# Attention scores and values in tiles of one shape: 64x32 for both, values in two banks

## The chip, the cores and the metric

The kernel runs on one core of a Trainium2 chip. Five engines work side by side, each through its own instructions in order: TensorE (PE in the profile; its weight loads are listed apart as PEld), VectorE (DVE), ScalarE (ACT), GpSimd (POOL) and SyncE (SP), which issues most DMAs. They meet at semaphores. TensorE writes its results to eight PSUM banks of 128 partitions x 512 f32; VectorE and ScalarE read them from there. The metric is the device time of one execution in microseconds, as the median of several runs.

## The reference

Two attention layers, a and b, of 32 heads of 20 features each over the same 2048 rows x of 640 features, with their own weights, and a gate for each row that mixes them.

```python
def _A_ref(x, wqkv, wo):
    B, S, D = x.shape            # 1, 2048, 640
    H = 32; Dh = D // H          # 20
    qkv = (lambda x, *d: x.transpose(*d))((x @ wqkv).reshape(B, S, 3, H, Dh), 2, 0, 3, 1, 4)
    q, k, v = qkv[0], qkv[1], qkv[2]
    scale = Dh ** -0.5
    scores = jnp.einsum("bhqd,bhkd->bhqk", q, k) * scale
    p = _softmax(scores, axis=-1)
    o = jnp.einsum("bhqk,bhkd->bhqd", p, v)
    return (lambda x, *d: x.transpose(*d))(o, 0, 2, 1, 3).reshape(B, S, D) @ wo
...
g = _sigmoid((x * gate_w).sum(-1, keepdims=True))
a = _A_ref(x, A_wqkv, A_wo)
b = _B_ref(x, B_wqkv, B_wo)
return g * a + (1 - g) * b
```

All inputs and the output are f32.

## The kernel before

The 64 heads of both layers go in 16 groups of four (GH = 4). For each group the queries come in four blocks of 512, and for each block the keys in eight pieces of 256: 16 x 4 x 8 = 512 steps. A group with a block of queries is called a unit here: eight steps.

In a step G the program does three kinds of work in turn, woven together by a string of letters (STEP, and LATE once no maxima are left):

- e: `scores` multiplies 128 keys of one head with 512 queries, in f16 (L696). Head j of a pair lies on partitions 64j to 64j + 63, so that two heads use the two row halves of TensorE, each product writing 128 partitions of one bank. ScalarE takes the exponential of the bank into an SBUF tile pt (L699). Eight products a step.
- m: `max_mm` computes scores once more, ahead of the steps (up to 15), the other way round: 128 queries with 512 keys, again f16 and on one row half (L638). VectorE reduces each bank to the largest score of each query (L649); for some of the products ScalarE first takes a positive part (L642) that VectorE then adds to the next bank while it reduces (L646). `finish_max` puts the negated maxima as extra rows beside the queries, so that the exponentials come out shifted. Eight products a step as well.
- V: `values` multiplies the weights pt of the step before, four heads, 128 keys, with the keys' values, in f32 (L714). Each head has 21 columns (20 features and a one, which sums the weights) and writes partitions 32h to 32h + 20 of the bank acc; the four heads lie side by side in four column tiles of TensorE. Two blocks V a step; acc gathers the 16 blocks of a unit.
- X: a slot for a piece of other work: projections of the next group, of the values, and of the output (`mms`, L426), with 128x128 tiles.

When a unit's last values are in, `take_acc` transposes acc on VectorE out of PSUM (L806), divides by the sum of weights (L811, L814), transposes back (L817) and stores the result in two f16 parts.

Of the eight banks one is acc, and seven (NB = 7) go in turns to everything else. `take` picks the one that is free first by a small clock in the program: `tick_score`, `tick_block` and `spend` carry an estimate of when TensorE, ScalarE and VectorE get to a piece of work, with T_SCORE for a pair of scores, T_VALUES for a block of values and T_MODE for what lies around a block. These numbers choose banks and nothing else; the order of the instructions is that of the program (manual_schedule), and each engine runs its own strictly in it.

Before the steps (now[0] < 0) the first group is projected and the maxima of its first two blocks of queries are computed.

Of the kernel before, what the change touches and what calls it, by code (L numbers as in the profile page):

```python
# [11 lines left out]
F32 = mybir.dt.float32  # L12
I32 = mybir.dt.int32
AF = mybir.ActivationFunctionType
OP = mybir.AluOpType
# [4 lines left out]
P = 128  # L20
# [4 lines left out]
NT = S // P  # L25
NC = D // P
GH = 4
NG = H // GH
GF = GH * DH
QB = 512  # L30
# [4 lines left out]
VW = DH + 1  # L35
# [23 lines left out]
AHEAD = 2  # L59
NB = 7  # L60

T_SCORE, T_MODE, T_VALUES, T_READY = 0.217, 0.1, 0.85, 0.39
T_EXP, T_MAX, T_BACK = 0.478, 0.6, 0.15
REST = 6
PRODUCT = "product"
# [6 lines left out]
def kernel(  # L72
# [10 lines left out]
    nc = tc.nc  # L83
# [7 lines left out]
    psum = ctx.enter_context(tc.tile_pool(name="psum", bufs=1, space=PSUM))  # L91
# [13 lines left out]
    QT = [consts.tile([P, 2, S], F16, name=f"qt{i}") for i in range(2)]  # L105
    KT = [consts.tile([P, 2, S], F16, name=f"kt{i}") for i in range(2)]

    KD = [consts.tile([P, 2, QB], F16, name=f"kd{i}") for i in range(2)]
    V = [consts.tile([P, NT, 2 * GH, VW], F32, name=f"v{i}") for i in range(2)]
    acc = psum.tile([P, QB], F32, name="acc")  # L110
    banks = [psum.tile([P, QB], F32, name=f"bank{i}") for i in range(NB)]
    gates = consts.tile([P, 2, NT], F32, name="gates")
    inv_x = consts.tile([P, 1], F32, name="inv_x")
    inv_g = consts.tile([P, 1], F32, name="inv_g")
# [16 lines left out]
    clock = {"pe": 0.0, "done": 0.0, "act": 0.0, "dve": 0.0}  # L131
    rows_free = [0.0, 0.0]
    block_end = [0.0, None]
    free_at, held = [0.0] * NB, set()
    now = [-1]
# [8 lines left out]
    def spend(engine, cost, ready=0.0):  # L144

        clock[engine] = max(clock[engine], ready) + cost
        return clock[engine] + T_BACK
# [5 lines left out]
    def tick_score(j, i):  # L153

        clock["pe"] = max(clock["pe"], rows_free[j], free_at[i])
        rows_free[j] = clock["pe"] + T_SCORE
        return clock["pe"] + T_READY

    def tick_block(cost, ready=0.0):

        begin = block_end[0] if now[0] < 0 and block_end[1] == rows_free else max(rows_free) + T_MODE
        clock["pe"] = max(begin, ready)
        rows_free[:] = [clock["pe"] + cost + T_MODE] * 2
        block_end[:] = [clock["pe"] + cost, list(rows_free)]
        clock["done"] = clock["pe"] + cost + T_READY - T_MODE
# [298 lines left out]
    def run(gen):  # L464
        for _ in gen:
            pass
# [142 lines left out]
    mparts, ready = {}, set()  # L609
# [12 lines left out]
    def max_mm(u, ch, heads=(0, 1)):  # L622

        g, qb, i = unit_of(u)
        pair, t = divmod(i, 4)
        if (g, qb) not in mparts:
            max_parts(g, qb)  # L630
        q0 = qb * QB + t * P
        for j in heads:
            two = u < AHEAD * NS or ch < 2 and (j == 0 or g == 0)
            i, pt = take()
            ready = tick_score(j, i)
            r = slice(64 * j, 64 * j + 60)
            k = KD[g % 2 if ch == 0 else 1][r, pair] if two and ch % 2 == 0 else KT[g % 2][r, pair, ch * QB:(ch + 1) * QB]
            nc.tensor.matmul(pt, QT[g % 2][r, pair, q0:q0 + P], k, start=True, stop=True)  # L638
            m = mparts[g, qb][:, pair, j, t, ch:ch + 1]
            if two and ch % 2 == 0:  # L640
                relus[u, j] = start.tile([P, QB], F32, name="rl0", bufs=4) if u < AHEAD * NS else work.tile([P, QB], F32, name="rl", bufs=2)
                nc.scalar.activation(relus[u, j], pt, AF.Relu)  # L642
                back = relu_at[u, j] = spend("act", T_EXP, ready)
            elif two:
                rl = relus.pop((u, j))
                nc.vector.tensor_tensor_reduce(rl, pt, rl, 1.0, LOW, OP.add, OP.max, m)  # L646
                back = spend("dve", T_MAX, max(ready, relu_at.pop((u, j))))
            else:
                nc.vector.tensor_reduce(m, pt, axis=AX.X, op=OP.max)  # L649
                back = spend("dve", T_MAX, ready)  # L650
            give(i, back)
# [26 lines left out]
    ptiles, weighed = {}, {}  # L678
# [9 lines left out]
    def scores(G, kk, pair, heads=(0, 1)):  # L688

        g, qb, i = unit_of(G)  # L690
        kt = 2 * i + kk
        for j in heads:
            i, et = take()
            ready = tick_score(j, i)
            r = slice(64 * j, 64 * j + 64)
            nc.tensor.matmul(et, KT[g % 2][r, pair, kt * P:(kt + 1) * P],  # L696
                             QT[g % 2][r, pair, qb * QB:(qb + 1) * QB], start=True, stop=True)
            pt = pp.tile([P, QB], F32, name="pt")
            nc.scalar.activation(pt, et, AF.Exp, scale=factor(g // 4))  # L699
            ptiles[G, kk, 2 * pair + j] = pt  # L700
            weighed[G, kk] = spend("act", T_EXP, ready)
            give(i, weighed[G, kk])
# [5 lines left out]

    def values(G, kk):
        g, qb, i = unit_of(G)  # L710
        tick_block(T_VALUES, weighed.pop((G, kk)))
        kt = 2 * i + kk
        for h in range(GH):
            nc.tensor.matmul(acc[32 * h:32 * h + VW, :], V[(g // 2) % 2][:, kt, (g % 2) * GH + h, :],  # L714
                             ptiles.pop((G, kk, h)), start=(kt == 0), stop=(kt == NT - 1))


    wo_parts = {}
# [83 lines left out]
    def take_acc(g, qb):  # L802


        turned = work.tile([P, QB], F32, name="ot", bufs=2)
        nc.vector.transpose(turned, acc)  # L806
        spend("dve", T_MAX)
        few, many = (2, 8) if g == 2 * NG - 1 else (6, 16)
        sq = work.tile([P, 16], F32, name="sq", bufs=2)
        t3 = turned.rearrange("p (b e) -> p b e", e=32)  # L810
        nc.vector.reciprocal(sq, t3[:, :, DH])  # L811
        spend("dve", 0.25)
        yield from turns(few)
        nc.gpsimd.tensor_tensor(t3, t3, sq.unsqueeze(2).to_broadcast([P, 16, 32]), op=OP.mult)  # L814
        yield from turns(many)
        ot = work.tile([P, QB], F32, name="ob", bufs=1)
        nc.vector.transpose(ot, turned)  # L817
        spend("dve", T_MAX)
        o = work.tile([P, 2, QB], F16, name="on", bufs=2)
        nc.gpsimd.tensor_copy(o[:, 0], ot)  # L820
        nc.gpsimd.tensor_tensor(o[:, 1], ot, o[:, 0], op=OP.subtract)
        if g < 2 * NG - 1:
            yield from turns(16)
            for h in range(GH):
                f = (g % NG * GH + h) * DH
                nc.sync.dma_start(o_scr[g // NG][:, f:f + DH, qb * QB:(qb + 1) * QB].rearrange("k d q -> d k q"),
                                  o[32 * h:32 * h + DH])
            stored.add((g, qb))
        else:
            last.append((qb, o))  # L830
# [16 lines left out]
    def take_last():  # L847

        ot = work.tile([P, QB], F32, name="ot", bufs=2)
        nc.scalar.activation(ot, acc, AF.Copy)  # L850
        i, pt = take()
        one = ident.rearrange("p (h e) -> p h e", e=32)[:, :, DH]
        for t in range(4):
            nc.tensor.matmul(pt[:, 4 * t:4 * t + 4], ot[:, t * P:(t + 1) * P], one, start=True, stop=True)
        busy(2)
        rc = work.tile([P, 16], F32, name="sq", bufs=2)
        nc.vector.reciprocal(rc, pt[:, :16])
        give(i, spend("dve", 0.3))
        i, pt = take()
        nc.tensor.transpose(pt[:16, :P], rc, ident)  # L860
        busy(2)
        rt = wts.tile([16, P], F32, name="rt", tag="rt", bufs=1)
        nc.scalar.activation(rt, pt[:16, :P], AF.Copy)
        give(i, spend("act", 0.3))
        o = work.tile([P, 2, QB], F16, name="on", bufs=2)
        rows_of = picks[0].rearrange("p k e -> p (k e)")
        spreads = []
        for t in range(4):
            spreads.append(take())
            nc.tensor.matmul(spreads[t][1][:, :P], rows_of[:, t * P:(t + 1) * P], rt, start=True, stop=True)  # L870
# [46 lines left out]
    start = start_stack.enter_context(tc.tile_pool(name="start", bufs=1))  # L917
# [3 lines left out]
    zeros = start.tile([P, QB], F16, name="zeros")  # L921
    nc.gpsimd.memset(zeros, 0.0)

    def clear(n):

        for _ in range(n):
            nc.tensor.matmul(acc, zeros[:, :P], zeros, start=True, stop=True)  # L927

    w_t = wqkv[0].rearrange("(c p) f -> p c f", p=P)
    for i in range(0, NT, 2):  # L930
# [164 lines left out]
    for block in range(AHEAD):  # L1095
# [7 lines left out]
            advance()  # L1103
        run(finish_max(0, block))
    run(rest)
    start_stack.close()

    pp = ctx.enter_context(tc.tile_pool(name="pp", bufs=12))
# [213 lines left out]
```

## Time and profile before

| | before |
|---|---|
| median of 3 runs | 2743.3 us (2743.12 to 2743.63) |
| span of the profiled execution | 2741.6 us |
| TensorE's granted clock | 1.00 in nearly all of the span |
| matmuls and weight loads in the trace | 23333 each |
| DMA | 46 GB/s on average |

Of the profiled execution the page gives the span, from its first to its last instruction; the runs' time includes what lies around it.

Times in the profile are in microseconds, and means of one instruction in ns. A row of groups reads: line, engine, operation, out<-in, shapes, count, then after the bar the time in which at least one of them ran, the mean length of one, and the idle time of the engine just before them with what ended it. In a timeline a row is start, length and what, with x8 for eight of a kind run together. An f32 product of the program stands in the trace as two matmuls and two weight loads. Matmuls overlap: one of 512 columns is listed with 0.38 us, though the next one in the same place can start after about 0.22.

The stages of the span: the start; from 103.6 us, the first block of values, the 512 steps, 468 of them between 190 and 2600 us; from 2665.6 us, the last reduction of maxima, steps without maxima until 2727.5 us; and the end.

### The profile page before, as it was taken

To read this page: it belongs to the slowest core of one execution; us is meant where nothing else is said; L and a number is where in the kernel's file an instruction comes from. 1 tells how busy PE (TensorE), PEld (TensorE's weight loads), DVE (VectorE), ACT (ScalarE), POOL (GpSimd) and SP (SyncE) were. 2 spreads that over 40 slices of the span, in tenths; PEclk is the share of its full clock that TensorE was granted. 3 is DMA by queue.
4 is the path that set the end of the run, shared out by engine and by line. 5 is a ranking of instruction groups with operands and counts; after the bars stand their busy time and mean duration, and the time that the engine had idled before them with its cause. 6 is when DMAs were issued, how large, how long until landed. Compare 5 with 4: busy or idle time off the path is not lost.

```text
span 2741.6 us, 62441 instructions
## 1 busy us (share of the span) xinstructions
PE 2725.5 (99%) x23333; PEld 940.2 (34%) x23333; DVE 2426.1 (88%) x4712; ACT 2533.9 (92%) x5149; POOL 699.6 (26%) x1010
## 2 busy tenths in 40 slices
PE   9999999999999999999999999999999999999999
PEld 4433333333333332333333333333333333333222
DVE  8789999999999999888888998989988888999992
ACT  4999999999999999999999999999999999999997
POOL 6232222222223422312221121223342212211111
PEclk9999999999999999999999999999999999999999
DMA  4021102010120211102012230221201112122112
GB/s 144 17 59 24 31 15 44 7 33 14 25 55 20 61 45 51 39 9 61 20 49 53 67 85 25 60 57 47 67 17 42 29 51 64 32 77 62 49 49 77
DMA packets 175401, 125.59 MB, mean 46 GB/s; under 512 B 103672, under 2 KB 145456, under 8 KB 175096
## 3 DMA queue, kind: packets, MB, share of 16 engines
q1 hardware_dynamic: 172552, 120.31, 17.2%
q8 instruction: 182, 2.98, 0.4%
q0 software_dynamic: 1600, 0.96, 0.3%
q14 instruction: 123, 1.01, 0.1%
q10 hardware_dynamic: 944, 0.33, 0.0%
HBM read 55.53 MB, written 31.86 MB: 32 GB/s over the span
## 4 chain that ended last, share of the span: by engine, by line
PE 96%; ACT 1%; DVE 1%; issue 0%; DMA 0%; POOL 0%; POOLq 0%; SPq 0%; ACTq 0%; DVEq 0%
PE acc L714 36%; PE bank L426 21%; PE bank L638 20%; PE bank L696 18%; ACT pt L699 1%; DVE mpart L649 1%; PE bank L895 0%; PE bank L956 0%; PE acc L927 0%; DMA xs<-in_A_x_dram 0%; DVE rl L646 0%; ACT rl L642 0%; DVE ot L806 0%; POOL xx L899 0%; POOL on L875 0%
## 5 line engine op out<-in xcount | busy, mean ns | idle before, releaser
L699 ACT ACTIVATE pt<-bank 128x512 f32<-128x512 f32 x4096 | 2167.1, 613 | 125.8 <-PE bank L696 91.6
L649 DVE TENSOR_REDUCE mpart<-bank 128x1 f32<-128x512 f32 x2944 | 1842.2, 681 | 227.3 <-PE bank L638 122.7
L714 PE MATMUL acc<-pt,v 128*21 128x512 f32 x8192 | 1081.7, 600 | 0.1
L696 PE MATMUL bank<-qt,kt 64*128 64x512 f16 x4096 | 1035.2, 380 | 1.4 <-ACT pt L699 0.9
L638 PE MATMUL bank<-kt,qt 60*128 60x512 f16 x3520 | 1006.7, 380 | 1.4 <-ACT pt L699 0.2
L638 PEld LDWEIGHTS <-qt 60*128 60x128 f16 x4096 | 237.9, 94 | 896.7 <-issue 829.3
L646 DVE CUSTOM_DVE_ANT_0 rl<-bank,rl 128x512 f32<-128x512 f32 x576 | 386.5, 677 | 7.2 <-ACT rl L642 2.8
L642 ACT ACTIVATE rl<-bank 128x512 f32<-128x512 f32 x576 | 339.0, 598 | 7.3 <-PE bank L638 6.7
L714 PEld LDWEIGHTS acc<-pt,v 128*21 128x21 f32 x8192 | 143.0, 99 | 429.5 <-issue 426.5
L696 PEld LDWEIGHTS <-kt 64*128 64x128 f16 x4096 | 229.4, 94 | 174.1 <-issue 64.1
L426 PE MATMUL bank<-xx,wbh 128*128 128x168 f16 (+3 forms) x2480 | 286.4, 236 | 0.6 <-DVE xx L961 0.3
L426 PE MATMUL bank<-xx,wbl 128*128 128x168 f16 (+3 forms) x1240 | 257.5, 235 | 0.0
L426 PEld LDWEIGHTS <-wbh 128*128 128x128 f16 x2480 | 192.5, 98 | 110.2 <-issue 104.6
L814 POOL TENSOR_TENSOR ot<-ot,sq 128x512 f32<-128x512 f32 x63 | 66.1, 1049 | 574.7 <-DVE sq L811 539.4
L638 PE MATMUL bank<-kd,qt 60*128 60x512 f16 x576 | 203.4, 379 | 0.8
L426 PE MATMUL bank<-woh,o_in 128*128 128x320 f16 (+3 forms) x700 | 157.7, 290 | 0.0
L426 PE MATMUL bank<-wvh,xx 128*128 128x160 f16 (+1 forms) x1280 | 156.6, 234 | 0.0
L455 POOL CAST cq<-fs 128x512 f16<-128x512 f32 x60 | 36.7, 611 | 459.9 <-ACT fs L453 459.9
L426 PEld LDWEIGHTS <-xx 128*128 128x128 f16 x1920 | 131.1, 97 | 59.0 <-issue 56.2
L426 PE MATMUL bank<-wvl,xx 128*128 128x160 f16 (+1 forms) x640 | 137.7, 232 | 0.0
L426 PEld LDWEIGHTS <-wbl 128*128 128x128 f16 x1240 | 121.2, 98 | 4.7 <-issue 1.3
L426 PEld LDWEIGHTS <-o_in 128*128 128x128 f16 (+1 forms) x1050 | 87.3, 97 | 91.0 <-issue 68.5
(156 smaller groups left out, 1288.6 us busy)
## 6 DMA issues: line engine op xcount, KB each, us to landing
y_scr<-y_out SPq DMA_DIRECT2D x48, 320.0 KB
y_out<-y_scr SPq DMA_DIRECT2D x32, 320.0 KB
kt<-cq SPq DMA_DIRECT2D x120, 80.0 KB
o_scr<-on SPq DMA_DIRECT2D x240, 40.0 KB
o_in<-o_scr SPq DMA_DIRECT2D x64, 96.0 KB
kt<-cq SPq DMA_DIRECT2D x136, 40.0 KB
wstage<-in_B_wqkv_dram SPq DMA_DIRECT2D x13, 400.0 KB
xs<-in_A_x_dram SPq DMA_DIRECT2D x8, 640.0 KB
```

Source lines behind the costliest of these rows:

```text
L426: nc.tensor.matmul(out_ap, a, b, start=(k == 0), stop=(k == len(pairs) - 1))
L455: nc.gpsimd.tensor_copy(hi, f)
L638: nc.tensor.matmul(pt, QT[g % 2][r, pair, q0:q0 + P], k, start=True, stop=True)
L642: nc.scalar.activation(relus[u, j], pt, AF.Relu)
L646: nc.vector.tensor_tensor_reduce(rl, pt, rl, 1.0, LOW, OP.add, OP.max, m)
L649: nc.vector.tensor_reduce(m, pt, axis=AX.X, op=OP.max)
L696: nc.tensor.matmul(et, KT[g % 2][r, pair, kt * P:(kt + 1) * P], QT[g % 2][r, pair, qb * QB:(qb + 1) * QB], start=True, stop=True)
L699: nc.scalar.activation(pt, et, AF.Exp, scale=factor(g // 4))
L714: nc.tensor.matmul(acc[32 * h:32 * h + VW, :], V[(g // 2) % 2][:, kt, (g % 2) * GH + h, :], ptiles.pop((G, kk, h)), start=(kt == 0), stop= ...
L814: nc.gpsimd.tensor_tensor(t3, t3, sq.unsqueeze(2).to_broadcast([P, 16, 32]), op=OP.mult)
```

## The change

The scores of the steps (both kinds, e and m) are written as four products of 32 columns of the stationary operand instead of one of 128, so that they run in tiles of 64 rows x 32 columns. The values' products are cut into two halves of 64 keys; the first half gathers in accs[0], the second in accs[1], so values run in 64x32 tiles too. At the end of a unit ScalarE copies accs[1] to SBUF, VectorE adds accs[0] to it, and the rest of take_acc follows. accs[1] is the seventh of the other banks until the steps begin; from then on six banks are left for the rest. The program's clock gets a new tick for values, without T_MODE.

```diff
-T_SCORE, T_MODE, T_VALUES, T_READY = 0.217, 0.1, 0.85, 0.39
+T_SCORE, T_MODE, T_VALUES, T_READY = 0.217, 0.1, 0.86, 0.39
...
-    acc = psum.tile([P, QB], F32, name="acc")
-    banks = [psum.tile([P, QB], F32, name=f"bank{i}") for i in range(NB)]
+    accs = [psum.tile([P, QB], F32, name=f"acc{i}") for i in range(2)]
+    banks = [psum.tile([P, QB], F32, name=f"bank{i}") for i in range(NB - 1)] + [accs[1]]
...
+    def product_of_score(pt, stationary, moving):
+
+        if now[0] < 0:
+            nc.tensor.matmul(pt, stationary, moving, start=True, stop=True)
+            return
+        for c in range(0, P, 32):
+            nc.tensor.matmul(pt[c:c + 32], stationary[:, c:c + 32], moving, start=True, stop=True)
+
+    def tick_values(ready):
+
+        clock["pe"] = max(max(rows_free), ready)
+        rows_free[:] = [clock["pe"] + T_VALUES] * 2
+        clock["done"] = clock["pe"] + T_VALUES + T_READY
...
-            nc.tensor.matmul(pt, QT[g % 2][r, pair, q0:q0 + P], k, start=True, stop=True)
+            product_of_score(pt, QT[g % 2][r, pair, q0:q0 + P], k)
...
-            nc.tensor.matmul(et, KT[g % 2][r, pair, kt * P:(kt + 1) * P],
-                             QT[g % 2][r, pair, qb * QB:(qb + 1) * QB], start=True, stop=True)
+            product_of_score(et, KT[g % 2][r, pair, kt * P:(kt + 1) * P], QT[g % 2][r, pair, qb * QB:(qb + 1) * QB])
...
-        tick_block(T_VALUES, weighed.pop((G, kk)))
+        tick_values(weighed.pop((G, kk)))
         kt = 2 * i + kk
-        for h in range(GH):
-            nc.tensor.matmul(acc[32 * h:32 * h + VW, :], V[(g // 2) % 2][:, kt, (g % 2) * GH + h, :],
-                             ptiles.pop((G, kk, h)), start=(kt == 0), stop=(kt == NT - 1))
+        pts = [ptiles.pop((G, kk, h)) for h in range(GH)]
+        for k, acc in enumerate(accs):
+            r = slice(64 * k, 64 * k + 64)
+            for h in range(GH):
+                nc.tensor.matmul(acc[32 * h:32 * h + VW, :], V[(g // 2) % 2][r, kt, (g % 2) * GH + h, :], pts[h][r],
+                                 start=(kt == 0), stop=(kt == NT - 1))
...
+        total = work.tile([P, QB], F32, name="ob", bufs=1)
+        nc.scalar.activation(total, accs[1], AF.Copy)
+        back = spend("act", T_EXP)
+        nc.vector.tensor_tensor(total, accs[0], total, op=OP.add)
+        spend("dve", T_MAX, back)
         turned = work.tile([P, QB], F32, name="ot", bufs=2)
-        nc.vector.transpose(turned, acc)
+        nc.vector.transpose(turned, total)
...
-        nc.scalar.activation(ot, acc, AF.Copy)
+        nc.scalar.activation(ot, accs[1], AF.Copy)
+        nc.vector.tensor_tensor(ot, accs[0], ot, op=OP.add)
...
+    held.add(NB - 1)
+    nc.tensor.matmul(accs[1], zeros[:, :P], zeros, start=True, stop=True)
     start_stack.close()
```

On TensorE, at a block of values in the middle of the program, the order before is this (names: qt queries, kt keys, v values; a score of kind m, the block with its four heads in one row, then scores of both kinds):

```order
L638 LDWEIGHTS qt_80
L638 MATMUL bank_92<-kt_82,qt_80 128x512
L714 MATMUL acc<-pt,v_87 21x512 x4
L638 LDWEIGHTS qt_80
L638 MATMUL bank_89<-kt_82,qt_80 128x512
L696 LDWEIGHTS kt_82
L696 MATMUL bank_90<-qt_80,kt_82 128x512
```

and with the change, at a like place (L165 is the line in product_of_score; acc_88 and acc_89 are the two banks of values):

```order
L165 LDWEIGHTS qt_80
L165 MATMUL bank_95<-kt_82,qt_80 32x512
L730 MATMUL acc_88<-pt,v_87 21x512 x4
L730 MATMUL acc_89<-pt,v_87 21x512 x4
L165 LDWEIGHTS qt_80
L165 MATMUL bank_90<-kt_82,qt_80 32x512
L165 LDWEIGHTS qt_80
L165 MATMUL bank_90<-kt_82,qt_80 32x512
```

Nothing changed its place; each score is four weight loads and four matmuls into quarters of its bank, one behind the other (the first two of bank_90 are shown), and the block of values has eight products instead of four.

On VectorE, around the end of a unit before, with what each waits for (L649 and L646 are maxima, L806 the transpose of acc):

```order
L649 TENSOR_REDUCE mpart<-bank_93 128x1 [waits PE_49]
L646 ISA rl,mpart<-bank_89,rl 128x512 [waits DVE_49,PE_49]
L646 ISA mpart 128x1
L806 STREAM_TRANSPOSE ot<-acc 128x512 [waits PE_49]
L811 RECIPROCAL sq<-ot 128x16 [waits DVE_49]
L649 TENSOR_REDUCE mpart<-bank_94 128x1 [waits PE_49]
```

and with the change (L824 is the sum):

```order
L660 ISA rl,mpart<-bank_90,rl 128x512 [waits DVE_49,PE_49,Activation_49]
L660 ISA mpart 128x1
L824 TENSOR_TENSOR ob<-acc_88,ob 128x512 [waits Activation_49]
L827 STREAM_TRANSPOSE ot<-ob 128x512 [waits DVE_49]
L832 RECIPROCAL sq<-ot 128x16 [waits DVE_49]
L663 TENSOR_REDUCE mpart<-bank_91 128x1 [waits PE_49]
```

The sum stands ahead of the transpose and waits for ScalarE where the transpose waited for TensorE. On ScalarE the copy has come between the exponentials (L712) at the same unit end:

```order
L712 ACTIVATE pt<-bank_95 128x512 [waits PE_49,Activation_49]
L712 ACTIVATE pt<-bank_93 128x512 [waits DVE_49,PE_49]
L822 ACTIVATE ob<-acc_89 128x512 [waits PE_49,Pool_49]
L712 ACTIVATE pt<-bank_94 128x512 [waits DVE_49,PE_49]
L712 ACTIVATE pt<-bank_92 128x512 [waits PE_49,Activation_49]
```

It waits for the unit's last values on TensorE, and everything behind it on ScalarE waits with it. SyncE and GpSimd have the same instructions in the same order as before.

More of the change, by code (lines that the diff above doesn't have):

```diff
@@ L926, in clear @@
         for _ in range(n):
-            nc.tensor.matmul(acc, zeros[:, :P], zeros, start=True, stop=True)
+            nc.tensor.matmul(accs[0], zeros[:, :P], zeros, start=True, stop=True)
     w_t = wqkv[0].rearrange("(c p) f -> p c f", p=P)
```

## The prediction

> **What bounds the kernel now.** I read the page first (span, busy time, the chain that ended last), then what TensorE waited for between 190 and 2600 us, where nearly all steps lie.
>
> ```profile
> span 2741.6 us, 62441 instructions
> ...
> PE 2725.5 (99%) x23333; PEld 940.2 (34%) x23333; DVE 2426.1 (88%) x4712; ACT 2533.9 (92%) x5149; POOL 699.6 (26%) x1010
> ...
> PE 96%; ACT 1%; DVE 1%; issue 0%; DMA 0%; POOL 0%; POOLq 0%; SPq 0%; ACTq 0%; DVEq 0%
> ...
> PE bank L696 <- ACT pt L699: 0.6, 2, 0.3
> ```
>
> The last row is the whole answer of the waits of PE in that window: 0.6 us in 2410. TensorE waits for nobody, and its own sequence sets the time. A busy PE is not a PE at its peak, though, so the next question is what its microseconds hold. The chain, piece by piece in order of time, shows one period of a step (start, length, what):
>
> ```profile
> 1199.12 0.99 PE acc L714 x8
> 1200.10 0.32 PE bank L638
> 1200.42 0.22 PE bank L696 x2
> 1200.64 0.00 PE bank L638
> 1200.64 0.22 PE bank L696 x2
> 1200.86 0.99 PE acc L714 x8
> ```
>
> Values take 0.99 us, the first pair of scores behind them 0.32, each later pair 0.22; the period is 1.74. To see what these would be without interruption I take a stretch of back-to-back matmuls of 512 columns from the start of the program:
>
> ```profile
> 11.16 10.52 PE L927 MATMUL acc<-zeros 128*128 128x512 f16 x48
> ...
> L927 PE MATMUL acc<-zeros 128*128 128x512 f16 x56 | 12.6, 379 | 0.0
> ```
>
> (10.52 - 0.38)/47 = 0.216 us for 512 f16 columns. A pair of scores, two row tiles side by side, is at that rate already. Values are two f32 passes, and eight records in two rounds of four:
>
> ```profile
> 1199.49 0.61 PE L714 MATMUL acc<-pt,v 128*21 128x512 f32 x4
> 1200.79 0.14 PEld L714 LDWEIGHTS acc<-pt,v 128*21 128x21 f32 x8 [0.43 <-issue]
> 1200.79 1.06 PE L714 MATMUL acc<-pt,v 128*21 128x512 f32 x8
> ```
>
> 1.06 - 0.61 = 0.45 us from round to round, so a pass costs about two columns' time per column, 2 x 0.216 = 0.43, and a block of values should be 0.86. Three pairs and one block should be 3 x 0.216 + 0.86 = 1.51 us; they take 1.74. **0.23 us per block of values is lost** where the array goes from 64x128 tiles to 128x32 tiles and back.
>
> Is that loss due to the tile shape, or to f16 against f32? The products of a projection are f16, as scores are, in one 128x128 tile:
>
> ```profile
> 1334.20 0.38 PE L638 MATMUL bank<-kt,qt 60*128 60x512 f16 x1
> 1334.51 0.24 PE L426 MATMUL bank<-wvh,xx 128*128 128x160 f16 x1
> ...
> 1335.43 0.23 PE L426 MATMUL bank<-wvl,xx 128*128 128x160 f16 x1
> 1335.50 0.23 PE L426 MATMUL bank<-wvh,xx 128*128 128x160 f16 x1
> 1335.66 0.39 PE L696 MATMUL bank<-qt,kt 64*128 64x512 f16 x1
> ```
>
> Score to projection 0.31 instead of 0.22, projection to score 0.16 instead of 0.07: 0.09 at each edge with one data type on both sides. So it is the shape.
>
> **The change part by part.** *Removed: the two edges of each block of values.* Scores and values both run in 64x32 tiles, so 0.23 us go at each of 8192/8 = 1024 blocks (L714's count in the period above, x8 each). I take 0.22, since eight tiles start one after the other: 0.02 us for four in the x4 row (0.61 against one matmul's 0.59 to 0.60), 0.007 each. 1024 x 0.22 = 225 us. TensorE alone would end at 2741.6 - 225 = 2517 us.
>
> *Split scores.* Sixteen score products of a step become 64. What I need is that four column tiles stream side by side at full rate. Values show it: four streams of 512 x 4 bytes in 0.43 us; four f16 streams of 512 x 2 bytes in 0.216 us are the same rate. A pair in 64x32 tiles is not in the trace. Lower bound: 0.216, nothing lost. Upper bound: the starts of eight tiles add to each round, 8 x 0.007 = 0.05, so 0.27; eight pairs a step then cost 0.4 us more, 512 x 0.4 = 205 us, which eats the gain: 2722. I take the lower end, because the second round of values follows the first after 0.45 with the starts of four tiles inside it.
>
> *Split values.* Two halves of 64 keys in two banks: eight products per block in place of four, but on eight tiles at once, 0.86 again. Bounds 0.86 to 0.86 + 4 x 0.007.
>
> *What is late next.* Without TensorE's edges the two engines behind it are close. The counts of the window 190 to 2600 us, and the time from one instruction to the next where they run back to back:
>
> ```profile
> L699 ACT ACTIVATE pt<-bank 128x512 f32<-128x512 f32 x3743 | 1983.7, 611 | 114.7 <-PE bank L696 82.3 <-PE bank L638 9.3
> L649 DVE TENSOR_REDUCE mpart<-bank 128x1 f32<-128x512 f32 x2805 | 1754.3, 681 | 205.2 <-PE bank L638 103.9 <-PE bank L696 96.5
> L714 PE MATMUL acc<-pt,v 128*21 128x512 f32 x7484 | 988.5, 600 | 0.0
> L646 DVE CUSTOM_DVE_ANT_0 rl<-bank,rl 128x512 f32<-128x512 f32 x469 | 316.6, 675 | 0.7 <-ACT pt L699 0.4 <-PE bank L638 0.2
> L642 ACT ACTIVATE rl<-bank 128x512 f32<-128x512 f32 x468 | 279.1, 596 | 0.9 <-PE bank L638 0.8
> L453 ACT ACTIVATE fs<-bank 128x128 f32<-128x128 f32 (+2 forms) x226 | 71.2, 315 | 15.8 <-issue 4.5 <-PE bank L426 3.3
> L806 DVE STREAM_TRANSPOSE ot<-acc 128x512 f32<-128x512 f32 x58 | 41.4, 714 | 3.4
> L817 DVE STREAM_TRANSPOSE ob<-ot 128x512 f32<-128x512 f32 x59 | 41.3, 699 | 0.0
> ...
> 511.43 1.09 ACT L699 ACTIVATE pt<-bank 128x512 f32<-128x512 f32 x2 [0.25 <-PE bank L696]
> 504.67 2.48 DVE L649 TENSOR_REDUCE mpart<-bank 128x1 f32<-128x512 f32 x4 [0.23 <-PE bank L638]
> ```
>
> 7484/16 = 468 steps in 2410 us, 5.15 each. TensorE would need 2410 - 936 x 0.22 = 2204. ScalarE: 1.09 - 0.61 = 0.48 per full tile, 4211 x 0.48 = 2021, with L453 and some 60 us of smaller groups about 2152. VectorE: (2.48 - 0.68)/3 = 0.60, 2805 x 0.60 + 317 + 83 = 2083, with some 75 us of smaller groups about 2158. Both stand within 3% of the new TensorE time, so the step comes near a balance of three engines, where each one's uneven moments reach the others.
>
> *Added.* At each of 63 unit ends (take_acc) a ScalarE copy of a bank, price 0.48 to 0.60 (L642, L699), and a VectorE sum of a bank and an SBUF tile. The trace has no such sum; between the 0.60 of a reduction and the 0.71 of L806 I take 0.68, as L646 reads the same two kinds of operand. That makes ScalarE about 2180 and VectorE about 2198 in the window. The sum waits for the copy and the copy for the values: behind the copy on ScalarE stand the exponentials of the next scores, behind the sum on VectorE the transpose, the reciprocal and the maxima. The next unit's first values wait for the sum. Does this reach TensorE? Before, at one unit end:
>
> ```profile
> 1201.92 0.72 DVE L806 STREAM_TRANSPOSE ot<-acc 128x512 f32<-128x512 f32 x1
> ...
> 1204.41 1.06 PE L714 MATMUL acc<-pt,v 128*21 128x512 f32 x8
> ```
>
> Values begin at 1200.79, VectorE reads them at 1201.92 and is done at 1202.64; the next values at 1204.41 leave 1.8 us. After: copy until 1202.5, sum until 1203.2, next values about 0.4 earlier, at 1204.0. Cover 0.8 us; it costs nothing while ScalarE is less than that behind.
>
> *Six banks in place of seven.* A unit end hands VectorE, beyond its maxima, the sum 0.68 and two transposes 1.4, with the small reductions about 2.6 us in one or two steps; spare time is some 0.1 us a step. What the banks do not absorb, TensorE waits. Lower end 0, upper end 63 x 2.6 = 164 us; there is no row that decides, and I take the middle, 82.
>
> *The sum:* 2517 + 82 = 2599 against the span of 2741.6. The runs' median is 2743.3, 1.7 us more, which lie around the span; as a run's time that is **2601**.
>
> **The rivals.** *The engines behind take most of it.* Same mechanism, nothing absorbed: 2517 + 164 = 2681. For it: one bank fewer, and three engines within about 1%. Against: the reductions' 205 us of idle time now.
>
> *The edges stay*, because a change from f16 to f32 within one shape drains too. Copies and sums lie beside TensorE, so about 2742. Against it: the 0.09 at f16 edges, the same size as half of 0.23.
>
> *Slower: TensorE's instructions come too slowly.* The place is the issue of weight loads and matmuls. A step now has 2 x (16 + 16 + 12.7) = 89 records in 5.15 us, and then 2 x (64 + 32 + 12.7) = 217, which in 4.7 us is one per 21.7 ns. In bursts TensorE does far better (eight weight loads in 0.14 us, each 0.10 long), but the densest longer stretch I find is this one, with 15 matmuls and 15 weight loads:
>
> ```profile
> 191.47 0.27 PE L426 MATMUL bank<-xx,wbh 128*128 128x128 f16 x2
> ...
> 192.25 0.22 PE L426 MATMUL bank<-xx,wbl 128*128 128x128 f16 x1
> ```
>
> 0.78 us for 30 records, 26 ns each, and there the columns set the pace. If 26 ns were the rate of issue, a step would be 217 x 0.026 = 5.64 us, 0.49 over 5.15: 2742 + 512 x 0.49 = 2993. It decides from 5.15/217 = 23.7 ns on. For it: nothing in this trace is that dense for long. Against it: the bursts.
>
> The Trainium skill, "TensorE: Matmul & The Clock Gate", Part 2, has a rule of this kind: where firmware and not the hardware decoder handles matmuls, each takes about 62 ns. By it a step's 64 + 16 + 12.7 = 93 matmul instructions would take 5.75 us, an estimate from that page, and the kernel about 3050. No row here shows which way matmuls are decoded.
>
> **How the numbers follow.** Forecast 2601: 0.58, own range 2520 to 2660. Engines behind, 2681: 0.16. Edges stay, or the split scores eat the gain, 2722 to 2742: 0.06, mostly within 0.2%. Issue, 2993: 0.20. Faster by over 0.2%: 0.58 + 0.16 + 0.01 = 0.75; within 0.2%, about what a measurement of this kernel tells from no change: 0.04; slower: 0.21. The range goes from 2520 (no wait behind TensorE) to 2760 (edges stay, and some waits); it leaves out the issue case, 0.20.
>
> **What would show it.** Right: in the chain, values and the pair behind them come to about 1.1 us in place of 1.31, pairs stay at 0.22, and waits of PE for banks appear, some 80 us, most near unit ends. ScalarE's and VectorE's shares rise to about 95%. Wrong: pairs longer than 0.24 with no wait named (tiles or issue); values over 0.95 with scores on both sides (the edge is not the shape); waits of PE above 160 us (balance worse than any unit end explains); values at unit ends waiting for the sum of take_acc.

## The result, and the profile after

The changed kernel takes 2904.0 us (median of 4 runs, 2903.2 to 2904.8) against 2743.5 us: a ratio of 1.058 (1.057 to 1.060). It is 160 us slower where 2601 us was forecast, and lies above the whole range given.

From the page of the changed kernel, in the order in which the rows of before were shown (span, busy time, the chain that ended last):

```profile
span 2901.9 us, 131228 instructions
...
PE 2831.2 (98%) x55718; PEld 1536.3 (53%) x55718; DVE 2470.8 (85%) x4776; ACT 2587.1 (89%) x5212; POOL 699.0 (24%) x1010
...
PE 79%; DVE 10%; ACT 7%; issue 3%; DMA 1%; POOL 1%; SPq 0%; DVEq 0%; ACTq 0%; POOLq 0%
```

The shares of VectorE and ScalarE fell (88% and 92% before) where they were to rise to 95%, and the chain now passes through both of them, 17% against 2%. Three engines wait for one another.

The groups of the window 190 to 2600 us, with idle time and what ended it behind the second bar:

```profile
L712 ACT ACTIVATE pt<-bank 128x512 f32<-128x512 f32 x3533 | 1898.2, 607 | 155.7 <-PE bank L165 113.6 <-ACT pt L712 9.0 <-DVE mpart L663 0.2
L663 DVE TENSOR_REDUCE mpart<-bank 128x1 f32<-128x512 f32 x2645 | 1654.0, 682 | 235.0 <-PE bank L165 201.1 <-ACT pt L712 24.9 <-ACT fs L467 3.6
L730 PE MATMUL acc<-pt,v 64*21 64x512 f32 x14128 | 1030.7, 591 | 0.0
L824 DVE TENSOR_TENSOR ob<-acc,ob 128x512 f32<-128x512 f32 x56 | 38.7, 692 | 61.5 <-ACT ob L822 61.5
L822 ACT ACTIVATE ob<-acc 128x512 f32<-128x512 f32 x56 | 35.2, 628 | 0.1
```

Values are 32 records a step now, so 14128/32 = 441.5 steps passed in 2410 us: 5.46 us a step, against 5.15 before and the 4.71 that the forecast needed. No instruction explains that: the exponentials take 607 ns and the maxima 682, as before (611 and 681); the sum takes 692 (0.68 us was put in) and the copy 628 (0.48 to 0.60).

The tiles themselves do what was forecast. The chain of the changed kernel, piece by piece (start, length, what):

```profile
1301.62 0.80 PE bank L165 x24
1302.41 0.86 PE acc L730 x16
1303.27 1.12 PE bank L165 x24
1304.39 0.86 PE acc L730 x16
```

A block of values takes 0.86 with scores on both sides, and no edge is left. But three pairs of scores, 0.65 without interruption, take 0.80 and 1.12. The timeline of the same place (start, length, what; x8 is two scores):

```profile
1301.99 0.42 PE L165 MATMUL bank<-kt,qt 60*32 60x512 f16 x8
...
1302.06 2.48 DVE L663 TENSOR_REDUCE mpart<-bank 128x1 f32<-128x512 f32 x4 [0.45 <-PE bank L165]
...
1302.21 1.06 PE L730 MATMUL acc<-pt,v 64*21 64x512 f32 x16
...
1303.03 3.17 ACT L712 ACTIVATE pt<-bank 128x512 f32<-128x512 f32 x6
1303.07 0.39 PE L165 MATMUL bank<-qt,kt 64*32 64x512 f16 x4
1303.09 0.40 PE L165 MATMUL bank<-kt,qt 60*32 60x512 f16 x4
...
1303.31 0.40 PE L165 MATMUL bank<-qt,kt 64*32 64x512 f16 x4
1303.39 0.40 PE L165 MATMUL bank<-kt,qt 60*32 60x512 f16 x4
...
1303.69 0.70 PE L165 MATMUL bank<-qt,kt 64*32 64x512 f16 x8
```

The four reductions start 0.60 apart ((2.48 - 0.68)/3), so they end at 1302.74, 1303.34, 1303.94 and 1304.54; the first exponential ends at 1303.64. Scores start at 1303.39, at 1303.69, and at 1303.99 (the second four of the x8 row, 0.70 - 0.40 behind the first). Each starts 0.05 us behind the end of a reader: TensorE has no free bank. In the window 190 to 2600 us 34% of the scores start 0.045 to 0.07 us behind an instruction of the engine that they wait for; before, 4% did. This is easily overlooked, because the list of waits gives TensorE almost nothing for it:

```profile
PE bank L165 <- ACT pt L712: 10.7, 36, 0.7
PE bank L165 <- DVE mpart L663: 9.7, 49, 0.2
```

20 us in 2410. A matmul is listed with 0.38 us though the next can follow after 0.22, so a wait of up to 0.16 us behind each pair lies under a busy TensorE. The waits have to be read from starts, or from the length of a step.

### The profile page after: what moved, and what is told of

Read it like the earlier page. It is cut to its first block, busy times and chain, and to the rows that moved or that the text cites. A ratio compares the mean times of both kernels' runs of the same rounds, so it can differ in the third digit from the quotient of the medians.

```text
span 2901.9 us, 131228 instructions
## 1 busy us (share of the span) xinstructions
PE 2831.2 (98%) x55718; PEld 1536.3 (53%) x55718; DVE 2470.8 (85%) x4776; ACT 2587.1 (89%) x5212; POOL 699.0 (24%) x1010
## 4 chain that ended last, share of the span: by engine, by line
PE 79%; DVE 10%; ACT 7%; issue 3%; DMA 1%; POOL 1%; SPq 0%; DVEq 0%; ACTq 0%; POOLq 0%
PE bank L165 35%; PE acc L730 25%; PE bank L440 17%; DVE mpart L663 8%; ACT pt L712 6%; PE bank L162 1%; ACT ob L822 1%; DMA ws<-in_A_wqkv_dram 0%; DVE rl L660 0%; PE bank L917 0%; ACT rl L656 0%; DVE ob L824 0%; DVE ot L827 0%; PE acc L440 0%; DVE wmax L293 0%
## 5 line engine op out<-in xcount | busy, mean ns | idle before, releaser
L712 ACT ACTIVATE pt<-bank 128x512 f32<-128x512 f32 x4096 | 2195.7, 610 | 190.7 <-PE bank L165 143.0
L165 PE MATMUL bank<-qt,kt 64*32 64x512 f16 x16384 | 1396.4, 379 | 26.3 <-DVE mpart L663 9.7
L730 PE MATMUL acc<-pt,v 64*21 64x512 f32 x16384 | 1196.3, 591 | 1.8 <-DVE ob L824 1.8
L165 PE MATMUL bank<-kt,qt 60*32 60x512 f16 x13824 | 1057.8, 380 | 17.0 <-ACT pt L712 5.5
L165 PEld LDWEIGHTS <-kt 64*32 64x32 f16 x16384 | 534.7, 90 | 577.4 <-issue 423.1
L165 PEld LDWEIGHTS <-qt 60*32 60x32 f16 x15872 | 481.7, 90 | 473.7 <-issue 355.1
L730 PEld LDWEIGHTS acc<-pt,v 64*21 64x21 f32 x16384 | 292.2, 95 | 44.8 <-DVE ob L824 2.1
L440 PE MATMUL bank<-xx,wbh 128*128 128x168 f16 (+3 forms) x2450 | 277.1, 234 | 2.9 <-ACT pt L712 0.3
L165 PE MATMUL bank<-kd,qt 60*32 60x512 f16 x2048 | 196.8, 379 | 3.9 <-DVE mpart L663 0.2
```

Of the source, the lines that this page charges most:

```text
L165: nc.tensor.matmul(pt[c:c + 32], stationary[:, c:c + 32], moving, start=True, stop=True)
L440: nc.tensor.matmul(out_ap, a, b, start=(k == 0), stop=(k == len(pairs) - 1))
```

## The experiments

### Taking the change apart

**One bank held back in the kernel before**, nothing else:

```diff
+    held.add(NB - 1)
```

> The kernel before with one of its seven banks held back for all of the steps; tiles, order and instructions as before. Theory B (banks: with six banks TensorE waits for ScalarE and VectorE to give banks back, and that outweighs the edges): 2850 us or more, waits of TensorE behind a bank's release grow from 87 us to several hundred. Theory T (tiles: the split scores are what is slow, the banks cost little): within 30 us of 2743.

Measured: 2876.5 us, ratio 1.049 (1.045 to 1.052). One bank of seven is worth 133 us in the old kernel, with the old tiles and with no copy and no sum.

**The change without the copy and the sum** (accs[1] is written and never read: the output lacks the second 64 keys of each block):

```diff
-        total = work.tile([P, QB], F32, name="ob", bufs=1)
-        nc.scalar.activation(total, accs[1], AF.Copy)
-        back = spend("act", T_EXP)
-        nc.vector.tensor_tensor(total, accs[0], total, op=OP.add)
-        spend("dve", T_MAX, back)
...
-        nc.vector.transpose(turned, total)
+        nc.vector.transpose(turned, accs[0])
...
```

> The changed kernel without ScalarE's copy and VectorE's sum at a unit's end; the second bank of values is filled and never read, so half of the keys are left out of the result. Theory S (the unit's end: VectorE's 75 us of waiting for the copy, and the 63 copies and sums, set the loss): 2780 us or less. Theory B and theory T: 2850 to 2895, since the split and the six banks stay.

Measured: 2809.4 us, 1.024 (1.021 to 1.027). Copy and sum, priced at nothing, cost 95 us.

**The new tiles with half of the values**: the first half only, in one bank, seven banks for the rest, no copy and no sum; the output lacks the second 64 keys of each block. And **the same with one bank held back**. Of the edit, the lines on the banks are shown.

```diff
-    accs = [psum.tile([P, QB], F32, name=f"acc{i}") for i in range(2)]
-    banks = [psum.tile([P, QB], F32, name=f"bank{i}") for i in range(NB - 1)] + [accs[1]]
+    accs = [psum.tile([P, QB], F32, name="acc")]
+    banks = [psum.tile([P, QB], F32, name=f"bank{i}") for i in range(NB)]
...
```

> The changed kernel with the first 64 keys of each block of values only (the other 64 are left out), one bank for values, no copy and no sum, and so seven banks for the rest; scores split as in the change, all in 64x32 tiles. Theory B: 2580 to 2680, TensorE without its edges and with its banks. Theory T: 2800 or more, since 64 score products a step are still there.

> As e3_half_7banks, with one of the seven banks held back during the steps: the two differ by one bank and nothing else. Theory B: slower than e3_half_7banks by 100 us or more, 2750 to 2880. Theory T and theory S: within 40 us of e3_half_7banks.

Measured: 2614.0 us, 0.953 (0.950 to 0.956), and 2797.7 us, 1.020 (1.017 to 1.023). With their bank the tiles with half of the values gain 130 us; the bank takes 184 back. Rows of values (16 a step in both), of the kernel with seven banks and of that with six:

```profile
L730 PE MATMUL acc<-pt,v 64*21 64x512 f32 x7920 | 1025.0, 589 | 0.0
```

```profile
L730 PE MATMUL acc<-pt,v 64*21 64x512 f32 x7332 | 952.0, 590 | 0.0
```

That is 495 and 458 steps in 2410 us, 4.87 and 5.26 us each. Of all pages, that of the one with seven banks shows the engines closest to one another:

```profile
PE 2585.3 (99%) x47525; PEld 1335.6 (51%) x47525; DVE 2396.4 (92%) x4712; ACT 2505.6 (96%) x5149; POOL 699.5 (27%) x1010
...
PE 92%; DVE 3%; ACT 2%; issue 1%; POOL 1%; DMA 1%; SPq 0%; POOLq 0%; ACTq 0%; DVEq 0%
```

These runs give the sum: 2743.5 - 130 (tiles, half of the values) + 184 (bank) + 12 (second half of the values, from 2797.7 to 2809.4) + 95 (copy and sum) = 2904. Taken in another order the parts could come out otherwise: the bank alone costs 133 us with the old tiles.

The 130 us are no price of the tiles alone. Half a block takes one row half of TensorE, and a score runs beside it on the other, between the two rounds of values, in the kernel with seven banks:

```profile
1302.11 0.60 PE L730 MATMUL acc<-pt,v 64*21 64x512 f32 x4
1302.12 0.38 PE L165 MATMUL bank<-kt,qt 60*32 60x512 f16 x4
1302.54 0.59 PE L730 MATMUL acc<-pt,v 64*21 64x512 f32 x4
```

In the change the second half stands there. What it would cost with seven banks is not shown: the 12 us were measured with six, where steps wait for banks anyway. And the kernel with seven banks waits for them too: 38% of its scores start 0.045 to 0.07 us behind an instruction of the engine that they wait for.

### What of the copy and the sum costs

**The copy without the sum**: the two lines of the sum are gone, VectorE transposes accs[0], and the second half is missing from the output.

> The changed kernel with ScalarE's copy at a unit's end and without VectorE's sum (VectorE transposes the first bank straight away, as in e2_no_sum; the second half of the keys is left out of the result). It stands between e2_no_sum (2809 us, neither) and the changed kernel (2904, both). Theory S1 (the price is VectorE waiting for the copy, and its sum): 2840 us or less. Theory S2 (the price is ScalarE, which waits for the values ahead of the copy and keeps its exponentials back): 2870 or more.

Measured: 2813.9 us, 1.026 (1.023 to 1.029). The copy on ScalarE costs 4 us; the other 90 come with VectorE's sum, its work and its wait for the copy.

**Both banks transposed by VectorE, the sum on GpSimd**: as much work on VectorE, no wait for ScalarE, and all keys in the output.

```diff
-        nc.scalar.activation(total, accs[1], AF.Copy)
...
-        nc.vector.tensor_tensor(total, accs[0], total, op=OP.add)
...
-        nc.vector.transpose(turned, total)
...
+        nc.vector.transpose(turned, accs[0])
...
+        nc.vector.transpose(other, accs[1])
...
+        nc.gpsimd.tensor_tensor(turned, turned, other, op=OP.add)
```

> The changed kernel with another sum: VectorE transposes both banks out of PSUM, GpSimd adds the two, ScalarE copies nothing; complete result. VectorE has 0.72 us for the second transpose in place of 0.69 for the sum, and waits for no copy. Theory S1 or S2 by waiting: 2830 to 2860 us. If it is VectorE's work alone that counts: 2890 or more.

Measured: 2852.9 us, 1.040 (1.037 to 1.043). The group of the second transpose in this kernel:

```profile
L825 DVE STREAM_TRANSPOSE ob<-acc 128x512 f32<-128x512 f32 x63 | 42.5, 674 | 0.0
```

2852.9 - 2809.4 = 43.5 us more for 42.5 us of VectorE. That fits the reading that what VectorE works more at a unit end reaches the end of the kernel, but doesn't prove it, since GpSimd's sum also moves what follows it. The remaining 2904.0 - 2852.9 = 51 us hold the copy's 4 and, by difference, VectorE's wait for it. In the list of waits of the changed kernel this wait is

```profile
DVE ob L824 <- ACT ob L822: 75.5, 63, 6.4
```

1.2 us at each of 63 unit ends, of which about 47 us, not quite two thirds, would come through.

**Is it the missing bank that makes the sum dear?** I supposed so, and put the same copy and sum into the kernel before:

```diff
+        total = work.tile([P, QB], F32, name="ob", bufs=1)
+        nc.scalar.activation(total, acc, AF.Copy)
+        back = spend("act", T_EXP)
+        nc.vector.tensor_tensor(total, acc, total, op=OP.add)
+        spend("dve", T_MAX, back)
...
-        nc.vector.transpose(turned, acc)
+        nc.vector.transpose(turned, total)
```

> The kernel before, seven banks, tiles as they were, with the same ScalarE copy and VectorE sum at each unit end. There is one bank of values, so the sum adds the copy to its own source: weighted values and sums of weights both double, and the quotient stays as it was. With the change the pair cost 95 us. Theory C, seven banks let TensorE run ahead through such a lump, as the prediction's cover said, and the cost of 95 us came with the sixth bank: 0 to 30 us more than before, 2743 to 2773 us. Rival D, VectorE's 0.69 us and its wait of 1.2 us at a unit end reach TensorE whatever the banks: 70 to 110 us more, 2813 to 2853 us. In between, the banks hide a part.

Measured: 2836.3 us, 1.034 (1.032 to 1.035), 93 us more than before. That theory falls: the pair costs the same with seven banks and the old tiles. A unit end of this kernel, VectorE's rows of the timeline:

```profile
1198.80 0.69 DVE L808 TENSOR_TENSOR ob<-acc,ob 128x512 f32<-128x512 f32 x1 [1.31 <-ACT ob L806]
...
1199.53 0.71 DVE L811 STREAM_TRANSPOSE ot<-ob 128x512 f32<-128x512 f32 x1
...
1200.44 3.61 DVE L649 TENSOR_REDUCE mpart<-bank 128x1 f32<-128x512 f32 x6
```

and of the kernel before, what follows the transpose that ended at 1202.64 in the prediction:

```profile
1202.84 3.68 DVE L649 TENSOR_REDUCE mpart<-bank 128x1 f32<-128x512 f32 x6
```

In both kernels six maxima stand in line behind the transpose and run back to back, without any idle time. Already before the change, TensorE had filled banks for VectorE by the time that a unit end was over; by this reading there was nothing left to absorb more. With the sum the line starts 1.31 + 0.69 us later, and TensorE runs out: the chain of this kernel at that place, cut to the pieces around its wait, reads

```profile
1200.80 0.98 PE acc L714 x8
...
1202.24 0.60 ACT pt L699
1202.85 0.04 issue
1202.89 0.37 PE bank L696
1203.26 0.99 PE acc L714 x8
```

2.46 us from values to values, against 1.74 in an undisturbed period. The chain names an exponential, whose end frees the bank for the next score; that it had to be this bank, because VectorE's line held the others, is my reading, as the trace doesn't list which bank is held when.

### The split scores by themselves

**The kernel before, with its scores in four 64x32 tiles** and its values in 128x32 tiles as they were:

```diff
+        for c in range(0, P, 32):
+            nc.tensor.matmul(pt[c:c + 32], stationary[:, c:c + 32], moving, start=True, stop=True)
...
```

> The kernel before with the steps' scores split into four 64x32 tiles and nothing else: values in 128x32 tiles in one bank, seven banks, the edges between two shapes stay. If a split score costs what an unsplit one does and 64x32 to 128x32 drains as 64x128 to 128x32 did: within 15 us of 2743. If the starts of eight tiles add 0.05 us to a pair (the upper bound of the prediction): 2940.

Measured: 2777.3 us, 1.012 (1.009 to 1.015), 34 us more, which neither expectation names. The timeline of TensorE in this kernel:

```profile
1400.23 1.06 PE L721 MATMUL acc<-pt,v 128*21 128x512 f32 x8
1401.22 0.40 PE L165 MATMUL bank<-kt,qt 60*32 60x512 f16 x4
...
1401.67 0.40 PE L165 MATMUL bank<-qt,kt 64*32 64x512 f16 x8
1402.00 1.06 PE L721 MATMUL acc<-pt,v 128*21 128x512 f32 x8
```

and in the kernel before:

```profile
1200.04 0.39 PE L638 MATMUL bank<-kt,qt 60*128 60x512 f16 x1
...
1200.48 0.38 PE L696 MATMUL bank<-qt,kt 64*128 64x512 f16 x2
1200.79 1.06 PE L714 MATMUL acc<-pt,v 128*21 128x512 f32 x8
```

Pairs follow after 0.22 to 0.24 in both (1401.22 to 1401.67 holds two, 0.45; before 1200.04 to 1200.48, 0.44). Values wait 0.33 behind the start of the last pair where they waited 0.31, and the period, 1400.23 to 1402.00, is 1.77 in place of 1.74. This place is above the usual: over all periods with three pairs between 190 and 2600 us the medians are 1.763 and 1.746, and 0.017 x 1024 makes 18 of the 34 us. The periods with projections, which hold an edge more, grow by 0.034 (3.474 against 3.440). So a score in four tiles makes an edge behind it dearer. With the change the edges at the blocks of values are gone, but those at the projections stay: up to about half of the 34 us is among its costs.

### How many banks a step needs

**A second bank held back in the kernel before**, and **banks given out strictly in turns**, with six and with seven:

```diff
-    held.add(NB - 1)
+    held.update((NB - 2, NB - 1))
```

```diff
-        i = min((k for k in range(NB) if k not in held), key=lambda k: free_at[k])
+        i = min((k for k in range(NB) if k not in held), key=lambda k: last_use[k])
+        last_use[i] = max(last_use) + 1
...
```

> The kernel before with two of the seven banks held back in the steps, five left (the first bank cost 133 us). Theory O, a bank is a matter of every step: a score holds its bank from its first product to the end of its reader, and with fewer banks the scores of every step wait for releases. The second bank then costs clearly more than the first, 250 to 500 us, so 3120 to 3380 us, and VectorE's waits for banks grow in all of the steps. Rival L, banks only absorb the lumps at the 63 ends of units, as the prediction sized them: at most 2.6 us each, 164 us in all, of which the first bank took 133; so at most 31 us more, up to 2910 us.

> The kernel before with six banks, which are given out strictly in turns (the free bank that was given out longest ago) and not by the program's estimate of which is free first. Theory O, the number counts: within 60 us of the run with six banks by the estimate (2876 us), and more likely above it than below. Rival C, the estimate picks badly once a bank is gone, and this is the cost: at least 60 us below it, 2740 to 2816 us.

> The same with all seven banks: the control for the run in turns with six. Theory O: the estimate is worth little where banks suffice, 2743 to 2800 us, and the difference from six to seven banks is again 100 to 190 us. Rival C: the difference from six to seven is below 60 us.

Measured: 3367.3 us with five banks, 1.227 (1.224 to 1.231); in turns 2921.6 us with six, 1.065 (1.062 to 1.068), and 2785.1 with seven, 1.015 (1.012 to 1.018). The first bank costs 133 us and the second 491, far more than 63 unit ends of 2.6 us could. In turns the seventh bank is worth 136.5 us, about what it is by the estimate (133): the number of banks counts, not a bad choice among those left. The page and the waits of the kernel with five banks:

```profile
PE 3106.6 (92%) x23333; PEld 979.0 (29%) x23333; DVE 2482.1 (74%) x4712; ACT 2603.3 (77%) x5149; POOL 698.1 (21%) x1010
```

```profile
PE bank L696 <- ACT pt L699: 143.7, 496, 0.6
```

Only here do many waits outgrow the length of a listed matmul and show in TensorE's own list. The groups of values, 190 to 2600 us, with six banks and with five (16 records a step):

```profile
L714 PE MATMUL acc<-pt,v 128*21 128x512 f32 x7124 | 941.0, 600 | 0.0
```

```profile
L714 PE MATMUL acc<-pt,v 128*21 128x512 f32 x6016 | 794.6, 600 | 0.0
```

| kernel | banks | us a step | banks x us |
|---|---|---|---|
| before | 7 | 5.15 | 36.1 |
| new tiles, half of the values | 7 | 4.87 | 34.1 |
| before, one held back | 6 | 5.41 | 32.5 |
| new tiles, half of the values, one held back | 6 | 5.26 | 31.6 |
| the change | 6 | 5.46 | 32.8 |
| before, two held back | 5 | 6.41 | 32.0 |
| the halves by turns (next section) | 6 | 5.85 | 35.1 |

Where banks are short, a step in the old order of the program takes about 32 bank-microseconds with either tiles; with six banks that is about 5.3 us. This is a figure of four kernels, not a law: another order needs more. The forecast's 4.71 x 6 = 28 lies below anything that a run reached.

Is it really every step, or mainly the unit ends? The starts of the blocks of values in the traces tell it. How much longer the eight steps of a unit get, each from the start of its first block to that of the next step (means of 58 steps, us):

| | 1 | 2 | 3 | 4 | 5 | 6 | 7 | 8 |
|---|---|---|---|---|---|---|---|---|
| old tiles, seven banks to six | 0.15 | 0.32 | 0.29 | 0.25 | 0.26 | 0.28 | 0.28 | 0.28 |
| old tiles, six banks to five | 1.11 | 0.92 | 0.98 | 1.03 | 1.01 | 0.97 | 0.99 | 0.91 |
| new tiles, half of the values, seven to six | 0.20 | 0.38 | 0.37 | 0.38 | 0.35 | 0.36 | 0.37 | 0.55 |
| copy and sum added, six banks | 0.58 | 0.00 | 0.00 | 0.00 | 0.00 | -0.01 | 0.00 | 0.85 |
| copy and sum added, old tiles, seven banks | 0.66 | 0.02 | 0.00 | 0.00 | 0.00 | 0.00 | 0.00 | 0.78 |

A missing bank makes all eight steps longer. Copy and sum cost at the unit end and nowhere else, and almost the same with six banks as with seven.

### Another order

**The two halves of the values by turns**, each on its row half of TensorE while scores run on the other, to spread the demand for banks. The scores of each kind stay the same, but their order changes too, so that those between V (first half) and W (second half) mostly run on the other row half. Banks, copy and sum are as in the change.

```diff
-STEP = ("e0 m0 m1 V m0 e1 e1 m0 m1 e1 e0 V e0 m1 m1 e0 e1 m0",
...
+HALF = "e1 V m1 e1 m1 e0 W m0 e0 m0"
+STEP = (f"{HALF} {HALF}", f"X {HALF} {HALF}", f"X {HALF} X {HALF}")
...
```

> The changed kernel in another order: the two halves of a block of values run one after the other, each on its own half of the array and into its own bank, beside scores on the other half, so that scores come evenly and not in bursts between blocks. Six banks, copy and sum as in the change; complete result. If banks are short because scores come in bursts (a block of values is 0.86 us without one): faster than the changed kernel by 60 us or more, 2700 to 2840. If six banks are too few for any order: 2880 or more.

Measured: 3095.4 us, 1.128 (1.125 to 1.131), the slowest complete form with six banks. A place in its timeline:

```profile
1402.45 1.80 ACT L711 ACTIVATE pt<-bank 128x512 f32<-128x512 f32 x3
...
1402.61 0.40 PE L164 MATMUL bank<-kt,qt 60*32 60x512 f16 x4
...
1403.10 0.40 PE L164 MATMUL bank<-qt,kt 64*32 64x512 f16 x4
1403.11 1.06 PE L730 MATMUL acc<-pt,v 64*21 64x512 f32 x8
```

The first exponential ends at 1403.05, and the score e0 starts 0.05 later. W, next in the program, needs no new bank, and with 0.22 us for a score its row half was free at 1402.83, behind the m1 of 1402.61; it starts at 1403.11, behind e0. Here a wait for a bank on one half held both back: W stands behind e0 in the program, and started behind it. How much of the 191 us over the change is this, I did not separate.

Halves by turns into one and the same bank, which would leave seven banks for the rest, wasn't tried. Both halves would write the same quarters of that bank, and no run here shows whether that goes right without a wait between them.

## Why the prediction was wrong, step by step

| step of the sum | predicted, us | measured, us |
|---|---|---|
| edges go, split scores and values at full rate (2517) | -225 | -130 (half of the values) |
| six banks for seven | +82 | +184 (133 in the old kernel) |
| second half of the values | 0 | +12 (with six banks) |
| copy and sum at 63 unit ends | 0 | +95 |
| sum | -143 | +161 |

- **The step that failed first is "Six banks in place of seven".** It counted only what a unit end hands to VectorE, 63 x 2.6 us at most, and so took for granted that in all the other steps six banks do. The runs show the opposite: a bank matters in every step (5.26 against 4.87 us on average, and longer at each of the eight places in a unit), and the price grows from 133 us for the first bank to 491 for the second. No row of the old profile gave it, as the text said; but then the upper end of 164 us wasn't a bound, since it was the price of one mechanism, and not of the resource. The Trainium skill, "TensorEngine Tiling (Array Packing)", "Gotcha 1: PSUM Pressure", says that row tiling asks more of PSUM, since row tiles at work side by side have to write different banks. It is by this rule that the two halves took a second bank. The runs show its price, 133 to 184 us; no run put both halves into one bank.
- **"Cover 0.8 us; it costs nothing" was wrong**, and not because of the banks. The cover was worked out for one waiter, the next unit's values, and these do indeed hardly wait (the sum kept them waiting once, 1.8 us in all). The waiter that counts is the line of six maxima behind the sum on VectorE, whose banks TensorE needs. The text names that line ("behind the sum on VectorE the transpose, the reciprocal and the maxima") and then doesn't follow it. Of the 95 us the copy itself is 4; the other 90 come with the sum, which the run with two transposes splits into some 43 for VectorE's work and some 47 of the 75.5 us of waiting. The wait alone was put at 0.6 us a unit end (1201.92 to 1202.5) and took 1.2. The loss stands in the last and the first step of a unit, 0.85 and 0.58 us.
- **The edges: mechanism right, gain smaller.** They go as forecast (0.86 in the chain), but with seven banks 130 of 225 us remain, and that with half of the values, beside which a score still ran; what all values would leave isn't shown. In that kernel scores wait for banks too, ScalarE is at 96% and VectorE at 92%, and 5% of the chain passes through them; this is the place that the rival "the engines behind" named, though not its price. How much of the missing 95 us each of these takes is open. Whether they would go with an eighth bank for scores, no run can show: one bank is needed for values.
- **Split scores at 0**: right for the pairs, which stay at 0.22. Of the 34 us of the split alone about half sit at edges that the change removes; those at the projections stay and were left out of the sum.
- **The rivals.** Slower came true, but not by the issue of instructions. The pairs before the values in the timeline of after (1301.99, eight matmuls and as many weight loads in 0.22 us) come to 14 ns a record, where the rival needed 24 or more. Over a longer stretch, the kernel without copy and sum gets from one block of values to the next, with three pairs between, in 1.62 us at best: 80 records, 20 ns each. Nor do the matmuls take the 62 ns each that the Trainium skill, "TensorE: Matmul & The Clock Gate", Part 2, gives for decoding in firmware: eight take 0.22 us. The edges did not stay. The mechanism that decided, every bank in use in every step, had no chance of its own; it stood as a term with a range too narrow.
- **The signs given** told it apart all the same: values 0.86 and pairs 0.22 where nothing waits, so tiles and issue were right; waits for banks everywhere, so the balance was wrong. Of these only some 20 us stand in TensorE's list, far under the 80 and 160 us named: the sign was right and the view wrong.

No version found beats the kernel before with all keys in its output. The best complete form of the change is the one with both transposes and GpSimd's sum, 2852.9 us.

## What to carry to other kernels

Before a change takes a buffer that everything passes through, hold one back in the old kernel and time it: one line, and it would have shown over half of the forecast gain to be gone, 133 of 225 us. Multiply buffers by the time of a step, and compare that before and after; a chain of 96% on one engine says nothing about spare buffers. When work is put ahead of a queue, the cover is the spare time of whoever waits for what stands behind it, not only that of the one that needs its result.

## What the runs showed of the hardware, unexpected

- A score that waits for a bank starts 0.05 us after the reader's last instruction on it has ended (1303.34 to 1303.39, 1303.94 to 1303.99), so the handing back itself is cheap. A product of 0.38 and a reader of 0.61 to 0.68 us make about 1.0 us; 32 bank-microseconds for 16 scores are 2.0, an upper figure, since projections use banks too. My reading of the difference is that banks mostly stand filled in line for their readers.
- Four f16 products of 32 columns side by side stream at the rate of one of 128 (pairs 0.22 apart), but what follows in another tile shape comes 0.02 us later behind the first start of a pair (0.33 against 0.31).
- Which free bank is taken is worth about as much as a small optimisation: giving them out in turns costs 42 us with seven banks and 45 with six.
